# A hand-written order of 1100 steps replaced by another: a gated mix of a long convolution and an MLP on one core

## The chip, the core and the metric

The kernel runs on one core of a Trainium2 chip. The core has five instruction streams of its own: TensorE (PE; its weight loads appear as PEld), VectorE (DVE), ScalarE (ACT), GpSimd (POOL) and SyncE (SP, which here issues nearly all DMAs). Each works through its own list in the order in which the program put it there, and waits by semaphores for the results of the others. The metric is the time on the device in microseconds (us), the median of the runs; a profile is one execution, and its span runs from the first instruction to the last.

## The reference

Inputs are bf16; S = 2048 positions, D = 640 channels, F = 1536. `q` serves as `x` for the second branch.

```python
def _A_ref(q, k, v, shift_k, ssm_k, ssm_D):
    k_pad = jnp.pad(k, ((0, 0), (ks - 1, 0), (0, 0)))
    for t in range(ks):                      # ks = 4
        k_shift = k_shift + k_pad[:, t:t + S, :] * shift_k[:, ks - 1 - t][None, None, :]
    kv = k_shift * v
    # y: convolution of kv with ssm_k along S, by FFTs of length 2*S
    y = y + kv * ssm_D[None, None, :]
    return q * y

def _B_ref(x, w1, w2, w3, w4):
    h = _gelu(_layernorm(x, axis=-1) @ w1)
    # four channel groups of h are shifted by +1, -1, +2, -2 positions -> hs
    x1 = x + hs @ w2
    return x1 + _gelu(_layernorm(x1, axis=-1) @ w3) @ w4

g = _sigmoid((x * gate_w).sum(-1, keepdims=True))
return g * a + (1 - g) * b
```

## The kernel before

Positions are tiled as 128 partitions by 16 (t1), so that four "chunks" c hold four t1 each. Both branches go through TensorE, and their steps are interleaved.

Branch A. `k_load` brings a chunk of k, transposes it by matmul (tile `pst`) and copies it out of PSUM; `tap` does the four-tap shift as matmuls with diagonal weights and multiplies by v, which `v_load` gathers by an indirect DMA on POOL. The long convolution is an FFT in four matmul steps. `step1` (a 64-point transform, L407 to L434) is run for the signal (KV) and for the kernel of the convolution (HT0), four chunks each: its PSUM tiles are copied into `stg` and sent to DRAM scratch (S_x and S_h). `gather` (L436) reads the scratch back transposed into an `ax` tile, `step2` (L446) does the second transform into XS and hs, `product` (L478) multiplies the spectra, `step3` (L493) transforms back, copies to `gs` and sends to S_g, `gin` (L524) reads that, and `step4` (L877) finishes, with the gate and the factor q.

Branch B. `x_stats` and `x_norm` do the first LayerNorm (bn_stats on DVE, the power on POOL, `row_order` the index rows of v), `x_turn` transposes by matmul (A or V letters) or by a DMA transpose (D). `mlp1` multiplies by w1, one of its groups (u = 4) by a regrouped copy W1M that `w1_mixed` (L201) makes on DVE from both halves of w1 (`load_w1`, tile WA); gelu runs on ACT. `h_shift` and `w2` (L776), then `x1_norm` (L797) with DMA transposes, `w3` (L833) with gelu, `w4` (L857) and `store` (L848). `z_rows` and `gate` make the gate.

Where a result leaves PSUM, `evac` (L354) copies it: on ACT with letter A (L356), on DVE with letter V (L358). The letters are part of the name of a step: `step1.HT0.0.VAAVVAVAVV` evacuates its ten tiles in turn by V, A, A, V and so on. `step4` and the norms have such letters too.

Nothing is left to a scheduler. All five engines run in the order in which the string `ORDER` lists the steps: 1100 entries "name.arguments:k", the k-th step of the named routine. `emit` takes them one by one, and what a step issues goes to the end of its engine's list. A step can belong to one engine or hold a DMA; so the place of an entry matters only against the other entries of the same engine, and against what it depends on.

```python
    def emit(names):
        for e in names:
            n, k = e.split(":")
...
    with tc.manual_schedule(engines={getattr(mybir.EngineType, n) for n in ("PE", "DVE", "Activation", "Pool", "SP")}):
        emit(ORDER)
```

The rings of tiles are set by hand as well. `SLOTS` has one digit for each allocation of a ring: "c" are the eight PSUM banks, "row" the four rows that stg, xn, gs and q2 share, "ax" the four gather tiles, and so on. A step that takes a slot waits until the last reader of the slot's former tile is done.

Of the kernel before, what the change touches and what calls it, by code (L numbers as in the profile page):

```python
# [41 lines left out]
def kernel(  # L42
# [24 lines left out]
        "c": "012345670124703510347205142356401723605162370514731057423671045261304732641374153670421350627413"  # L67
             "502634751264351270361427503164257364102546173045621537426107432715604371401362570164301257613045"
             "267236057416537621507362651374026372401534762501373150427102547535706432073125640736450750634127"
             "504763270415367204325170635147630125460327156034215760147362304167135620316425031672301402715320"  # L70
             "1724107361761423564023714053627501267420674256271306234",
        "row": "01230213021302320123012031203120310310303",
        "gt": "012301031010231012301201",
        "xt": "010101",
        "gq": "0120201201021020120122102121021021",
        "ax": "0123120312030213",
        "hp": "01231302",
# [798 lines left out]
    def step4(t1, ev):  # L876
# [26 lines left out]
        def total():  # L903
# [170 lines left out]
                 f1_table=f1_table, t2_table=t2_table, i_tables=i_tables, f4_table=f4_table, kv_alloc=kv_alloc, k_load=k_load, k_wrap=k_wrap, v_load=v_load, tap=tap,  # L1074
                 kv_consts=kv_consts, mlp1=mlp1, load_h=load_h, h_transpose=h_transpose,
# [50 lines left out]
```

## Time and profile before

| | |
|---|---|
| median of 3 runs | 229.23 us (229.17 to 229.64) |
| span of the profiled execution | 225.9 us |
| around the span (median less span) | 3.3 us |
| instructions | 6037 |
| PE busy | 217.5 us, 96% of the span |
| DVE busy | 192.4 us, 85% |
| ACT busy | 173.0 us, 77% |
| POOL busy | 16.3 us, 7% |
| DMA | 57.62 MB, mean 255 GB/s |

The profiled execution has no time of its own beside its span; the median of the runs is taken for it. Busy times of PE are modelled: a matmul that is held up between two others counts as busy. Names such as `ps<-ax,CMP` mean output from inputs. A "releaser" is what ended a wait.

### The profile page before, as it was taken

Reading aid. Unit: us, or ns where it says so; the run is one execution under the profiler, and the core shown is the slowest. Engines: PE = TensorE matmul, PEld = TensorE weight load, DVE = VectorE, ACT = ScalarE, POOL = GpSimd, SP = SyncE. Lnnn points to the kernel's source line nnn. Section 1 sums busy time; section 2 is a strip of 40 time slices with the busy share of each in tenths; the row PEclk is TensorE's granted clock in tenths of the full one; section 3 lists DMA queues with packets and bytes.
Section 4 is the critical chain, followed back from the end, with each engine's and each line's share of the span. In section 5 each row is a group of like instructions: output and inputs, shape, how many; then the busy total and the mean of one; then the engine's idle time right before and its main releaser. Section 6 shows DMA issues by size and latency. Waiting matters only on the chain.

```text
span 225.9 us, 6037 instructions
## 1 busy us (share of the span) xinstructions
PE 217.5 (96%) x2419; PEld 120.4 (53%) x2420; DVE 192.4 (85%) x500; ACT 173.0 (77%) x344; POOL 16.3 (7%) x34
## 2 busy tenths in 40 slices
PE   8979989999999999999999999999999999999994
PEld 2557555436846554344664445555533547657762
DVE  7899999999999999873999998989999841439994
ACT  4799988989989989999977597967988450266450
POOL 3238020000000200010400000000000000000000
PEclk9999999999999999999999999999999999999999
DMA  6999997964998999999999560592695779418915
GB/s 238 381 362 336 308 249 193 344 282 104 392 352 353 307 240 290 376 361 369 300 250 303 121 232 4 156 361 70 69 323 195 219 269 372 189 30 321 310 77 197
DMA packets 43841, 57.62 MB, mean 255 GB/s; under 512 B 20514, under 2 KB 36514, under 8 KB 43558
## 3 DMA queue, kind: packets, MB, share of 16 engines
q1 hardware_dynamic: 43238, 54.62, 75.3%
q0 software_dynamic: 576, 2.62, 3.1%
q8 instruction: 19, 0.31, 0.6%
q14 instruction: 8, 0.07, 0.1%
HBM read 34.94 MB, written 18.36 MB: 236 GB/s over the span
## 4 chain that ended last, share of the span: by engine, by line
PE 63%; DMA 16%; DVE 15%; issue 1%; ACT 1%; SPq 1%; ACTq 0%
PE ps L864 23%; PE ps L837 18%; DMA WA<-in_B_w_dram 5%; DMA W<-in_B_w_dram 5%; PE ps L461 4%; PE ps L890 4%; PE psw L785 4%; PE psm L703 4%; DMA ax<-S_x 4%; PE ps L508 3%; DMA S_h<-stg 3%; PE ps L419 2%; DVE KV L601 2%; DVE KV L598 2%; DVE HT L358 2%; DVE HM L758 1%
## 5 line engine op out<-in xcount | busy, mean ns | idle before, releaser
L837 PE MATMUL ps<-x1t,W 128*128 128x512 bf16 x240 | 56.1, 380 | 0.0
L864 PE MATMUL ps<-W,gt 128*128 128x320 bf16 (+2 forms) x383 | 55.1, 299 | 0.6 <-DMA W<-in_B_w_dram 0.5
L864 PEld LDWEIGHTS <-gt 128*128 128x128 bf16 x384 | 36.2, 98 | 18.3 <-issue 2.8
L841 ACT ACTIVATE gt<-ps 128x512 bf16<-128x512 f32 x48 | 27.6, 609 | 19.0 <-PE ps L864 10.6
L837 PEld LDWEIGHTS <-W 128*128 128x128 bf16 x240 | 21.8, 98 | 28.2 <-issue 5.5
L356 ACT CAST stg<-ps 128x512 bf16<-128x512 f32 x55 | 28.6, 608 | 3.0 <-PE ps L419 1.8
L867 DVE SCALAR_TENSOR_TENSOR X<-ps,OMG,X 128x320 bf16<-128x320 f32 (+2 forms) x32 | 17.2, 548 | 11.9 <-PE ps L864 11.7
L703 PE MATMUL psm<-xt,WA 128*128 128x512 bf16 x100 | 23.4, 379 | 1.2 <-DMA WA<-in_B_w_dram 1.1
L356 ACT CAST gs<-ps 128x320 bf16<-128x320 f32 x41 | 15.6, 439 | 8.7 <-PE ps L508 5.2
L785 PE MATMUL psw<-WA,HT 128*128 128x320 bf16 x116 | 21.3, 299 | 0.2
L358 DVE CAST XS<-ps 128x512 bf16<-128x512 f32 x19 | 12.5, 684 | 5.3 <-PE ps L461 5.3
L356 ACT CAST hs<-ps 128x512 bf16<-128x512 f32 x28 | 15.0, 606 | 1.9 <-PE ps L461 1.9
L358 DVE CAST stg<-ps 128x512 bf16<-128x512 f32 x25 | 15.9, 683 | 0.2
L703 PEld LDWEIGHTS <-WA 128*128 128x128 bf16 x100 | 9.2, 97 | 12.0 <-DMA WA<-in_B_w_dram 1.2
L785 PEld LDWEIGHTS <-HT 128*128 128x128 bf16 x116 | 10.9, 98 | 7.7 <-issue 4.1
L894 ACT ACTIVATE y<-ps,GS 128x320 bf16<-128x320 f32 x22 | 10.4, 526 | 5.7 <-PE ps L890 3.5
L788 DVE SCALAR_TENSOR_TENSOR X<-psw,X 128x320 bf16<-128x320 f32 x32 | 14.2, 483 | 0.1
L358 DVE CAST gs<-ps 128x320 bf16<-128x320 f32 x23 | 10.7, 485 | 2.4 <-PE ps L508 1.7
L706 ACT ACTIVATE HT<-psm 128x512 bf16<-128x512 f32 x20 | 11.6, 618 | 1.2 <-PE psm L703 1.1
L356 ACT CAST XS<-ps 128x512 bf16<-128x512 f32 x21 | 11.9, 609 | 0.5 <-PE ps L461 0.3
L785 PE MATMUL psw<-WA,HM 128*128 128x320 bf16 x44 | 12.3, 299 | 0.0
L794 ACT ACTIVATE jk<-X 128x640 bf16<-128x640 bf16 x16 | 12.1, 759 | 0.0
(145 smaller groups left out, 334.8 us busy)
## 6 DMA issues: line engine op xcount, KB each, us to landing
S_x<-stg SPq DMA_DIRECT2D x8, 640.0 KB
S_h<-stg SPq DMA_DIRECT2D x8, 640.0 KB, 3.4
ax<-S_x SPq DMA_DIRECT2D x8, 640.0 KB, 8.1
ax<-S_h SPq DMA_DIRECT2D x8, 640.0 KB, 6.0
S_g<-gs SPq DMA_DIRECT2D x8, 640.0 KB, 3.6
W<-in_B_w_dram SPq DMA_DIRECT2D x2, 1920.0 KB
kn<-in_A_k_dram SPq DMA_DIRECT2D x4, 640.0 KB
E<-in_A_ssm_k_dram SPq DMA_DIRECT2D x5, 512.0 KB
```

The lines of the kernel that those rows point to most:

```text
L356: A.copy(out=dst, in_=src)
L358: V.tensor_copy(out=dst, in_=src)
L703: PE.matmul(ps[:].rearrange("p (a b) -> p a b", a=4), lhsT=W1N[:, k, 160 * u:160 * u + P] if u < 4 else W1M[:, k, :], rhs=xt[:, :, k, :], ...
L706: A.activation(out=st["HT"][:, 4 * c:4 * c + 4, u, :], in_=ps[:].rearrange("p (t b) -> p t b", t=4), func=ACT.Gelu_apprx_tanh)
L785: PE.matmul(ps[:], lhsT=h_tile(f, t1), rhs=W2P[:, f, o:o + W], start=(f == 0), stop=(f == 4))
L788: V.scalar_tensor_tensor(out=X1[:, t1, o:o + W], in0=box["ps"][:], scalar=1.0, in1=X[:, t1, o:o + W], op0=ALU.mult, op1=ALU.add, accum_out ...
L794: A.activation(out=jk[:], in_=X1[:, t1, :], func=ACT.Square, accum_out=S12[:, 1, t1:t1 + 1])
L837: PE.matmul(ps[:].rearrange("p (a b) -> p a b", a=4), lhsT=st["W3"][:, k, f * P:(f + 1) * P], rhs=xt[:, :, k, :], start=(k == 0), stop=(k ...
L841: A.activation(out=st["gt", c, f // 4][:, f % 4, :], in_=ps[:], func=ACT.Gelu_apprx_tanh)
L864: PE.matmul(ps[:], lhsT=st["gt", c, f // 4][:, f % 4, i * P:(i + 1) * P], rhs=st["W4"][:, f, o:o + w], start=(f == 0), stop=(f == FC - 1))
L867: V.scalar_tensor_tensor(out=X1[:, t1, o:o + w], in0=box["ps"][:], scalar=OMG[:, t1:t1 + 1], in1=X1[:, t1, o:o + w], op0=ALU.mult, op1=ALU ...
L894: A.activation(out=box["y"][:], in_=box["ps"][:], func=ACT.Copy, scale=GS[:, t1:t1 + 1])
```

## The change

The strings `ORDER` and `SLOTS` are replaced; all other lines are the same, but those behind ORDER move down by eight. The 1100 steps issue the same arithmetic and the same DMAs. What differs: the order on each of the five engines, the digits of the ring slots, and the letters of some steps, which move an evacuation between L356 (ACT) and L358 (DVE), a norm between ACT and DVE, or a step4 half between its two forms (L894 with L897, or L900). Counted over the whole program, DVE gets 39 copies of 128x512 in place of 44, 8 of step1.HT0's shape in place of 12 and 21 of 128x320 in place of 23. ACT gets four loads of its function table in place of five.

At the front, on POOL `v_load.1` and `v_load.3` now stand between the first power of `x_stats` and the second, `v_load.0` behind the second and `v_load.2` behind the third, where all four stood behind the second; `w1_mixed` comes forward to stand behind `x_stats.1`; w1, x2 and all of k are asked for early; `pow0` goes to the end. In the middle step1.HT0.1 and `load_w4` come earlier among the steps. At the end six step4 tiles (8 to 13) are finished directly before `w4.14`, the last product, and the stores 1, 7, 5, 6 and 4 lie among them.

The diff, cut to its core:

```diff
     SLOTS = {
...
-        "row": "01230213021302320123012031203120310310303",
-        "ax": "0123120312030213",
...
+        "row": "01023103302123013210321031331312301211210",
+        "ax": "0123102301232310",
...
     ORDER = (
-        "open.L1.left:0 open.A2.right:0 consts0:0 load_x0.0:0 warm:0 load_x0.1:0 consts0:1 warm:1 warm:2 pow0:0 "
-        "kv_alloc:0 k_load.3.AVA:0 f4_table:0 x_stats.0.VVVA:0 warm:3 k_load.3.AVA:1 x_stats.0.VVVA:1 load_x.1:0 "
-        "x_stats.0.VVVA:2 k_load.3.AVA:5 x_stats.0.VVVA:3 x_stats.0.VVVA:4 x_stats.0.VVVA:5 x_stats.0.VVVA:6 warm:4 "
-        "row_order:0 k_load.2.VAV:0 f1_table:0 x_norm.0.VVAA:0 x_norm.0.VVAA:1 f4_table:1 x_stats.1.VVVV:0 "
-        "k_load.3.AVA:2 load_x.3:0 x_norm.0.VVAA:2 x_stats.1.VVVV:1 k_load.3.AVA:3 x_turn.0.AAA:0 k_load.3.AVA:6 "
-        "k_load.2.VAV:5 load_w1.1:0 x_norm.0.VVAA:3 k_load.2.VAV:1 x_stats.1.VVVV:2 x_turn.0.AAA:1 x_stats.1.VVVV:3 "
-        "x_turn.0.AAA:2 x_stats.1.VVVV:4 load_w1.0:0 x_stats.1.VVVV:5 x_stats.3.VVAA:0 k_load.3.AVA:4 x_norm.1.VVVV:0 "
-        "x_turn.0.AAA:4 k_load.2.VAV:3 x_turn.0.AAA:3 x_turn.0.AAA:5 x_stats.3.VVAA:1 x_norm.1.VVVV:1 x_norm.1.VVVV:2 "
-        "v_load.2:0 k_load.0.AAV:0 f1_table:1 mlp1.0.2:0 mlp1.0.3:0 x_norm.1.VVVV:3 v_load.0:0 k_load.1.AVV:0 "
-        "k_load.2.VAV:6 mlp1.0.0:0 load_x.2:0 x_stats.3.VVAA:2 x_turn.1.VVV:0 x_turn.1.VVV:4 mlp1.0.1:0 "
-        "x_stats.3.VVAA:3 x_turn.1.VVV:1 k_load.2.VAV:4 x_stats.3.VVAA:4 x_stats.3.VVAA:5 k_load.0.AAV:3 x_turn.1.VVV:5 "
-        "mlp1.0.3:1 x_stats.3.VVAA:6 x_turn.1.VVV:2 v_load.3:0 x_turn.1.VVV:3 k_load.1.AVV:3 w1_mixed:0 v_load.1:0 "
-        "mlp1.0.0:1 x_stats.2.VVAA:0 mlp1.0.2:1 k_load.0.AAV:1 mlp1.0.1:1 x_stats.3.VVAA:7 k_load.0.AAV:5 mlp1.1.2:0 "
-        "x_norm.3.VVVV:0 x_norm.3.VVVV:1 k_load.0.AAV:4 load_cj:0 k_load.0.AAV:2 mlp1.1.2:1 x_norm.3.VVVV:2 "
-        "x_norm.3.VVVV:3 x_stats.2.VVAA:1 k_load.1.AVV:5 mlp1.0.4:0 k_load.1.AVV:4 mlp1.0.4:1 k_load.1.AVV:1 d_fold:0 "
-        "mlp1.1.4:0 x_turn.3.D:0 kv_consts:0 x_stats.2.VVAA:2 mlp1.1.0:0 k_load.2.VAV:2 k_wrap:0 k_load.1.AVV:6 "
...
-        "step2.x.3.AVVVVVAAVA:7 step2.x.0.VAVVAVAAVA:10 w3.0.11:1 w3.0.3:1 step1.HT0.1.VVAAAAAAVA:15 x1_norm.1.VVAA:3 "
...
-        "step2.x.3.AVVVVVAAVA:8 load_w4:0 w3.0.1:1 scale_x1.4.V:0 step2.x.0.VAVVAVAAVA:12 w3.0.2:1 w3.0.8:1 "
...
-        "step4.9.VV:2 w4.15:0 step4.11.AA:2 step4.12.AA:0 step4.10.AA:3 step4.14.AV:4 step4.14.AV:1 step4.8.VA:1 "
-        "load_q.3:0 step4.14.AV:5 step4.11.AA:5 step4.14.AV:2 store.1:0 step4.13.AA:0 store.2:0 step4.12.AA:3 "
-        "step4.8.VA:2 step4.15.AA:5 step4.15.AA:1 step4.14.AV:6 step4.15.AA:2 step4.12.AA:1 step4.10.AA:4 store.0:0 "
-        "step4.9.VV:6 step4.13.AA:3 step4.12.AA:2 step4.13.AA:4 step4.10.AA:0 step4.8.VA:4 step4.10.AA:5 store.3:0 "
-        "w4.13:2 step4.11.AA:6 w4.15:1 step4.12.AA:4 step4.13.AA:5 w4.15:2 step4.8.VA:5 w4.13:3 step4.10.AA:1 "
-        "step4.8.VA:6 step4.10.AA:2 step4.13.AA:1 step4.10.AA:6 w4.14:0 step4.13.AA:2 w4.15:3 step4.12.AA:5 store.4:0 "
-        "step4.13.AA:6 store.5:0 step4.15.AA:6 step4.12.AA:6 store.7:0 store.6:0 w4.14:1 w4.14:2 w4.14:3 store.8:0 "
-        "store.8:1 close.L2:0 close.C:0"
+        "open.L1.left:0 open.A2.right:0 consts0:0 kv_alloc:0 warm:0 consts0:1 f4_table:0 f4_table:1 row_order:0 "
+        "load_x0.0:0 x_stats.0.VVVA:0 load_x0.1:0 load_x.3:0 x_stats.0.VVVA:1 k_load.0.VAV:0 warm:1 "
+        "x_stats.0.VVVA:2 warm:2 warm:3 warm:4 load_x.1:0 x_stats.0.VVVA:3 x_stats.0.VVVA:4 f1_table:0 "
+        "k_load.0.VAV:5 k_load.2.AAV:0 x_stats.0.VVVA:5 k_load.0.VAV:3 x_stats.0.VVVA:6 load_w1.0:0 "
+        "x_stats.3.VVAA:0 x_stats.3.VVAA:1 x_stats.3.VVAA:2 x_stats.3.VVAA:3 load_w1.1:0 k_load.0.VAV:1 "
+        "x_stats.3.VVAA:4 x_stats.3.VVAA:5 x_norm.0.VAAA:0 x_stats.1.VVVV:0 x_norm.0.VAAA:1 x_norm.0.VAAA:2 "
+        "load_x.2:0 k_load.3.VAV:0 x_stats.1.VVVV:1 x_stats.1.VVVV:2 k_load.1.AVV:0 d_fold:0 x_stats.1.VVVV:3 "
+        "x_turn.0.AAA:0 k_load.2.AAV:5 v_load.1:0 load_cj:0 x_norm.0.VAAA:3 w1_mixed:0 k_load.2.AAV:1 "
+        "x_stats.1.VVVV:4 x_turn.0.AAA:1 v_load.3:0 k_load.0.VAV:2 x_turn.0.AAA:4 x_turn.0.AAA:5 x_turn.0.AAA:2 "
+        "x_turn.0.AAA:3 k_load.2.AAV:3 k_load.2.AAV:4 k_load.0.VAV:4 f1_table:1 mlp1.0.0:0 mlp1.0.0:1 "
+        "x_stats.1.VVVV:5 mlp1.0.4:0 x_stats.3.VVAA:6 x_stats.2.VVAA:0 x_norm.1.VVVV:0 x_norm.1.VVVV:1 "
+        "x_norm.1.VVVV:2 x_norm.1.VVVV:3 v_load.0:0 mlp1.0.2:0 mlp1.0.2:1 mlp1.0.4:1 load_h.0:0 k_load.3.VAV:5 "
+        "k_load.3.VAV:6 x_stats.2.VVAA:1 k_load.0.VAV:6 x_turn.1.VAV:0 x_turn.1.VAV:1 x_turn.1.VAV:4 x_turn.1.VAV:5 "
+        "k_load.2.AAV:2 x_stats.2.VVAA:2 x_stats.3.VVAA:7 x_norm.3.VVVV:0 x_norm.3.VVVV:1 x_norm.3.VVVV:2 "
+        "x_norm.3.VVVV:3 kv_consts:0 load_gw:0 x_turn.1.VAV:2 x_turn.1.VAV:3 x_stats.2.VVAA:3 x_stats.2.VVAA:4 "
+        "k_load.3.VAV:1 k_load.3.VAV:2 x_turn.3.D:0 x_stats.2.VVAA:5 x_stats.2.VVAA:6 k_load.1.AVV:1 v_load.2:0 "
...
+        "step2.x.3.VVVAVAAVAV:9 x1_norm.1.VVVA:2 step1.HT0.1.AAVVAVAAAA:15 w3.0.7:1 scale_x1.2.V:0 "
...
+        "step2.x.3.VVVAVAAVAV:5 x1_norm.1.VVVA:5 load_w4:0 w4.0:0 w4.3:0 step2.x.3.VVVAVAAVAV:4 "
...
+        "step4.2.AV:3 step4.6.AV:2 step4.6.AV:6 step4.2.AV:4 gin.1.1:0 gin.1.0:0 step4.2.AV:5 store.0:0 store.3:0 "
+        "w4.15:0 step4.15.VV:1 store.2:0 w4.15:1 step4.3.AA:3 step4.3.AA:4 step4.2.AV:6 step4.3.AA:5 w4.15:2 "
+        "step4.15.VV:2 step4.15.VV:6 step4.3.AA:6 w4.12:2 w4.15:3 w4.12:3 step4.10.AV:0 store.1:0 step4.10.AV:3 "
+        "step4.10.AV:4 store.7:0 step4.12.AA:3 step4.10.AV:1 step4.8.VA:0 step4.10.AV:5 step4.8.VA:1 step4.10.AV:2 "
+        "step4.8.VA:2 step4.11.AA:3 step4.12.AA:4 step4.12.AA:5 step4.11.AA:0 step4.10.AV:6 step4.11.AA:4 "
+        "step4.11.AA:5 step4.12.AA:0 step4.9.AA:3 step4.11.AA:1 step4.11.AA:2 step4.12.AA:1 step4.12.AA:2 "
+        "step4.11.AA:6 step4.13.AA:0 store.5:0 step4.13.AA:1 step4.13.AA:2 step4.12.AA:6 step4.9.AA:0 step4.8.VA:3 "
+        "step4.13.AA:3 step4.13.AA:4 step4.13.AA:5 step4.9.AA:1 step4.9.AA:2 step4.13.AA:6 store.6:0 step4.8.VA:4 "
+        "step4.8.VA:5 step4.9.AA:4 step4.9.AA:5 step4.8.VA:6 step4.9.AA:6 store.4:0 w4.14:0 w4.14:1 w4.14:2 "
+        "store.8:0 w4.14:3 store.8:1 close.L2:0 close.C:0"
     ).split()
```

More of the change, by code (lines that the diff above doesn't have):

```diff
@@ L66 @@
     SLOTS = {
[L67 to L71, printed above, removed]
-        "row": "01230213021302320123012031203120310310303",
-        "gt": "012301031010231012301201",
-        "xt": "010101",
-        "gq": "0120201201021020120122102121021021",
-        "ax": "0123120312030213",
-        "hp": "01231302",
+        "c": "012034567373207230175236075104632571023647601574231635410276451730207453215646054317234053721604"
+             "165704150742063145273604123106425731750436120716274306251643510723570416256201547364532156360172"
+             "714601421645030162714367406314254160327320150137613457275436245613157060142537127630145467236717"
+             "632021453520616240357137056564170324037156573120401465230541726713474641237612450241354351506270"
+             "2516056073751540613470132546301256075670617056170261570",
+        "gt": "000010223300203102301201",
+        "row": "01023103302123013210321031331312301211210",
+        "xt": "011101",
+        "gq": "012012020220210202222102102102",
+        "ax": "0123102301232310",
+        "hp": "01232031",
     }
```

280 rows, old and new, of the table ORDER are left out of this document.

## The prediction

> **What bounds the kernel now.** I read the page's first lines, then the busy time by stages, then the chain, and only then single stretches.
>
> ```profile
> span 225.9 us, 6037 instructions
> ...
> PE 217.5 (96%) x2419; PEld 120.4 (53%) x2420; DVE 192.4 (85%) x500; ACT 173.0 (77%) x344; POOL 16.3 (7%) x34
> ...
> PE 63%; DMA 16%; DVE 15%; issue 1%; ACT 1%; SPq 1%; ACTq 0%
> ```
>
> The median is 229.23 us and the span 225.9, so some 3.3 us lie around the span; I add them to every sum. "PE 96%" tempts one to say that TensorE bounds all of it and that no new order can matter. The chain says otherwise: 31% of the span goes back to DMA and DVE. The windows (span, then busy us and count of PE, PEld, DVE, ACT, POOL, then granted clock, DMA share, GB/s) show where:
>
> ```profile
> 0.00:10.00 10.00, 8.92 (x38) 3.75 (x39) 7.88 (x41) 5.65 (x9) 3.53 (x15) 1.00 0.80 303
> 10.00:30.00 20.00, 17.74 (x269) 11.73 (x270) 19.09 (x64) 19.94 (x38) 6.60 (x9) 1.00 1.03 321
> 30.00:60.00 30.00, 29.18 (x478) 16.75 (x466) 28.79 (x86) 26.53 (x52) 1.32 (x2) 1.00 0.78 260
> 60.00:78.00 18.00, 17.69 (x129) 9.78 (x127) 17.57 (x61) 16.86 (x33) 1.21 (x2) 1.00 0.91 337
> 78.00:90.00 12.00, 11.88 (x79) 6.41 (x77) 11.74 (x39) 11.18 (x23) 0.00 (x0) 1.00 1.09 277
> ...
> 180.00:200.00 20.00, 20.00 (x150) 11.42 (x149) 6.94 (x16) 5.08 (x11) 0.00 (x0) 1.00 0.66 247
> ```
>
> From 10 to 90 us DVE is busy 77.2 of 80 us: it sets the pace there, with ACT close behind. After that PE is the fullest, and from 180 to 200 DVE and ACT have almost nothing to do. PE's busy time before 90 us is stretched: a matmul that waits for its PSUM bank between two others counts as busy. So I put PE on an axis of its own work instead.
>
> ```profile
> 3.55 11.11 DMA WA<-in_B_w_dram
> 14.70 3.41 PE psm L703 x15
> 18.11 0.67 PE pst L615 x12
> 18.78 1.08 PE psm L703 x5
> ...
> 126.72 1.63 PE ps L864 x12
> ...
> 222.12 1.02 DVE X L867 x2
> ```
>
> Unhindered, five matmuls of L703 take 1.08 us and twelve of L864 1.63 (start, length, what, in the chain); likewise for the other forms. Counted over the order, PE's work is 206.5 us, the same in both programs. The last matmul ends at 222.1, so PE has lost 222.1 − 206.5 = 15.7 us by then, and DVE and stores add 3.8. The loss grows unevenly: by the row of 14.70 it is 3.0 us; at the w3 group at 87.14 (axis 77.6) it is 9.5; at the first w4 matmul, 105.71, it is 12.1; the rest comes in small pieces.
>
> ```profile
> 86.60 0.60 PE L419 MATMUL ps<-HT,F 64*128 64x512 bf16 x4
> 87.14 1.25 PE L837 MATMUL ps<-x1t,W 128*128 128x512 bf16 x5
> ...
> 105.71 0.58 PE L864 MATMUL ps<-W,gt 128*128 128x320 bf16 x3 [0.51 <-DMA W<-in_B_w_dram]
> ```
>
> The 9.5 have a simple reading. Around axis 79 PE needs results that stand behind 6.3 us more DVE work than PE has done itself; what remains, 9.5 − 6.3 = 3.2 us, is time that DVE idled on the way (2.1 of it before 10 us, by the first window). So the loss at that point is DVE work ahead plus DVE idle time, and these two I follow into the changed order.
>
> **The change part by part.** The instructions are the same but for the engines of some evacuations.
>
> *Evacuations moved.* DVE copies 11 tiles fewer out of PSUM at L358 (stg, XS, hs, gs), ACT as many more at L356. With the smaller exchanges of letters, each at its row's mean, DVE loses 5.9 us of work and ACT gains 3.7; ACT also drops one of five table loads.
>
> ```profile
> L356 ACT CAST stg<-ps 128x512 bf16<-128x512 f32 x55 | 28.6, 608 | 3.0 <-PE ps L419 1.8 <-ACT jk L794 0.7 <-DMA S_h<-stg 0.3
> ...
> L358 DVE CAST stg<-ps 128x512 bf16<-128x512 f32 x25 | 15.9, 683 | 0.2
> ```
>
> Most of that falls after 100 us, where the evacuations run beside PE and cost nothing. What counts is the DVE work ahead of PE in the paced part. There the tightest point becomes w3.0.6 at axis 77.1, which needs w2.14 behind 82.7 us of DVE work: 5.6 ahead, where it was 6.3. That is −0.7. ACT, in exchange, gets 32 of the 40 evacuations of step1.HT0, where it had 28 (step1.HT0.0 alone goes from 4 to 9), and its own work ahead of PE goes from 0.1 us at axis 59.5 to 0.9 at 78.2. While DVE is 5.6 ahead and late besides, ACT is covered; I count 0, and the four moved copies at 608 ns, 2.4 us, as the other end if that cover goes (second rival).
>
> *The front.* Now v_load.1 and v_load.3 stand on POOL right behind the first pow, ahead of the second, and w1_mixed stands on DVE right after x_stats.1.
>
> ```profile
> 7.45 1.03 POOL L653 TENSOR_TENSOR RS<-VE,EXPO 128x4 f32<-128x4 f32 x1 [4.55 <-DVE pf L256]
> ...
> 16.07 1.20 POOL L172 DMA_INDIRECT KV<-in_A_v_dram,ROWS  x1 [0.17 <-issue]
> ```
>
> The traffic of queue 0 (packets, MB, share), what the trace has on the tile of W1 (WA), and the use of W1 on DVE:
>
> ```profile
> q0 software_dynamic: 576, 2.62, 3.1%
> ```
> ```profile
> L196 SPq DMA_DIRECT2D WA<-in_B_w_dram x2: 939/1206/1474, 3.5 to 4.5; - x2
> ...
> DMA to landing us min/median/max: 11.2/11.2/11.2
> ```
> ```profile
> 21.41 0.32 DVE L202 COPY WA<-WA 128x640 bf16<-128x640 bf16 x1
> ```
>
> So these gathers start at about 10 us instead of 16 (the pow ends at 8.5, ROWS takes 0.3, a gather 1.2). Each moves a quarter of 2.62 MB, and at the 321 GB/s of 10 to 30 us two of them are 4.1 us of traffic. W1's halves are issued at 3.5 and 4.5 and take 11.2 us, so they land at 14.7 and 15.7 and are under way just then. In the old order w1_mixed ran at 21.41, long after W1; in the new one it stands behind 13.6 us of DVE work, so with the idle 2.1 it is reached at 15.7, when W1 has only just come by the old timing. DVE then waits between 0 (W1 served first) and 4.1 us (the gathers served first). I take 2.3, an even sharing: over the 4.6 us that follow 10 us, half goes to the gathers. Behind w1_mixed on DVE wait the x_norm, tap and evacuation work of the whole paced part, so this idle time adds directly to 3.2: it is **+2.3**. x2, k3 and k1 are all issued early and share the same engines; their lateness lies inside the same bounds.
>
> [...]
>
> *W4 and the first gathers.*
>
> ```profile
> 94.93 1.41 SPq L215 DMA_DIRECT2D W<-in_B_w_dram  x1
> ```
> ```profile
> 92.53 0.59 PE L837 MATMUL ps<-x1t,W 128*128 128x512 bf16 x2
> 93.24 0.85 PE L461 MATMUL ps<-ax,CMP 64*32 64x384 bf16 x48
> ```
>
> W4 is issued at 94.93 behind S_h sends that end step1. In the new order that last step1 and W4's issue come about 2 us earlier against PE, so the 0.51 wait goes (end of the row at 105.71). Between the two rows at 92.53 and 93.24 PE also loses some 0.3 us (two matmuls of L837 need 2 × 1.08/5 = 0.43 of the 0.71) to the first gather of S_x, which the new order issues earlier too: −0.8 in all, 0 to −0.8. The S_h gathers behind it get tighter. Between the release of an ax slot and its first use PE has 5.4 us of work for h.6, 6.2 for h.0, 6.5 for x.4, 7.6 for h.7 and 8.3 for h.5, where all had 7.9 to 13.8 before. A gather takes this long:
>
> ```profile
> DMA to landing us min/median/max: 6.0/7.0/8.1
> ```
>
> At 6.0 only h.6 is short, by 0.6; at 7.0 h.6, h.0 and x.4 are short by 1.6 + 0.8 + 0.5 = 2.9. PE stretches a little in that time, so I take **+1.0** (0 to 2.9).
>
> *The tail.* Six step4 tiles now stand right before w4.14: 12 half tiles, 3.3 us of PE, and 10 of them go over ACT:
>
> ```profile
> L894 ACT ACTIVATE y<-ps,GS 128x320 bf16<-128x320 f32 x22 | 10.4, 526 | 5.7 <-PE ps L890 3.5 <-DVE q L897 1.9
> ```
>
> That is 5.3 us of ACT against 3.3 of PE. Up to eight PSUM banks absorb the difference; the last w4 may wait for one: **+0.3** (0 to 1). The last step3 and its sends end about 5 us later than before (190 against 185), which the nearly empty DVE and ACT of 180 to 200 cover; first use is at about 200.
>
> Sum: −0.7 + 2.3 − 0.8 + 1.0 + 0.3 = +2.1, and 225.9 + 2.1 + 3.3 = 231.3 us. PE's work of 206.5 is equal in both, so a loss can come back only by less lag, and the paced part sets that.
>
> **The rivals.**
> *The front holds (faster).* W1 lands at 14.65 and 15.7 as before, because the gathers get what is left. Then w1_mixed waits for nothing, the −0.7 and −0.8 stand, the S_h gathers cost 0 to 0.6 (the lower landing time), and the tail 0 to 0.3: −1.5 to −0.6, 227.7 to 228.6; if a tenth of the 5.9 us that DVE sheds shortens the path elsewhere (from 60 to 78 us DVE is busy 17.57 of 18), 227.2. For it: the DMA engines in the first window are busy only 0.80. Against it: from 10 to 30 us it is 1.03 already. It decides if W1's second half lands before 15.7. Chance 0.27.
> *ACT becomes the bound.* From 60 to 78 us ACT is already busy 16.86 of 18 us, so it has 1.1 to spare, and two of the four moved copies fill that. If the front has held it as well, the whole 2.4 stands behind DVE's lateness and not beside it: 231.3 + 2.4 = 233.7. For it: 19.94 busy of 20 from 10 to 30. Against it: a late DVE gives ACT time. Chance 0.22.
> *Nothing comes of it.* The evacuations of the paced part wait for PE and the other way round, so shifts are taken up, so that PE's 206.5 meets about the old lag: the gains (−1.5) against a half-sized front (+1.2) give 228.9, within 0.45 of before. Chance 0.06.
> The forecast, 229.8 to 232.5 by the front's 0.8 to 3.5, keeps 0.45.
>
> **How the numbers follow.** A difference of 0.2% (0.45 us) is what a measurement can tell here. Faster takes the first rival, 0.27; the same 0.06; slower is the forecast and the ACT rival, 0.67. The range runs from the low end of the first rival, 227.2, to the ACT rival with part of what the gather term (2.9 instead of 1.0) or W1 (4.1 instead of 2.3) can add, 235.0. The forecast's own range stands above.
>
> **What would show it.** Right: DVE waits 1.5 to 3 us for WA at L202 near 16 us; the first w4 matmul comes without a wait for W, PE waits for ax appear at L461 for S_h gathers, the lag at the w3 group of axis 77 is 10 to 11 us. Wrong: no DVE wait at L202, and a lag there under 9 (first rival); ACT busy over 17.5 of 18 us in the stretch before that group with DVE waiting for ACT (second); a last matmul at 222 with all of these (third). Above all it would be wrong if a transfer that I took as early is late in a stage I counted as covered, such as S_g before 200 us.

## The result and the profile after

The changed kernel takes 237.47 us, the median of 4 runs (236.37 to 238.2), against 229.38 us (229.17 to 229.64) for the kernel before: a ratio of 1.0347, 95% interval 1.0311 to 1.0383. The forecast was 231.3 us with a range up to 235.0. The direction was right, the size was not. The profiled execution took 237.79 us.

The first lines of the page of the changed kernel, its granted clock in 40 slices, and the chain by engine:

```profile
span 236.0 us, 6047 instructions
...
PE 222.6 (94%) x2420; PEld 122.3 (52%) x2420; DVE 187.8 (80%) x489; ACT 176.9 (75%) x350; POOL 16.8 (7%) x34
...
PEclk9979999799999999999999999999999999999999
...
PE 73%; DMA 13%; DVE 9%; issue 2%; SPq 1%; DVEq 0%
```

The span is 10.1 us longer, the median only 8.1. Here 237.79 − 236.0 = 1.8 us lie around the span, and 1.7 to 1.9 in the other runs whose span and time are both on record, not the 3.3 that the prediction took from the median less the span. So the profiled execution of before was most likely faster than its median, by some 1.5 us, and as much of the differences between the two traces may be the spread of executions. The forecast is best compared as a span: 228.0 forecast, 236.0 measured.

The page already shows two things that the forecast did not hold: two slices in which the clock dips, and DVE, whose share falls by 5 points although its work falls by only 4.6 us. The prediction's axis, PE's own work, shows where the time goes. The table gives PE's lag behind that axis, worked out from the start of each group of matmuls in the two traces:

| axis, us of PE work | lag before | lag after | difference |
|---|---|---|---|
| 9.5 | 0.9 | 2.25 | 1.35 |
| 17 | 3.0 | 6.15 | 3.15 |
| 23 | 2.9 | 6.8 | 3.9 |
| 30 | 4.0 | 10.9 | 6.9 |
| 36 | 4.55 | 13.1 | 8.55 |
| 48 | 6.6 | 16.1 | 9.5 |
| 77 | 9.4 | 19.3 | 9.9 |
| 102 | 12.5 | 22.3 | 9.8 |
| 150 | 15.3 | 25.15 | 9.85 |
| 204 | 16.1 | 25.8 | 9.7 |

The whole loss is there before axis 77; behind it nothing is lost or won on balance. PE comes to axis 77 at some 96.2 us, in the kernel before at some 86 (its last window ends at 85.8, axis 76.4; DVE does not idle in between). Up to there the windows of the changed kernel (span, then busy us and count of PE, PEld, DVE, ACT, POOL, granted clock, DMA share, GB/s) are:

```profile
0.00:10.00 10.00, 9.01 (x43) 4.05 (x43) 7.88 (x41) 6.22 (x14) 1.87 (x12) 1.00 0.82 298
10.00:30.00 20.00, 16.20 (x140) 10.39 (x139) 16.93 (x58) 18.47 (x30) 8.63 (x12) 0.91 1.09 343
30.00:50.00 20.00, 16.81 (x443) 9.15 (x442) 14.40 (x33) 13.14 (x26) 0.38 (x2) 0.91 0.71 211
50.00:96.20 46.20, 45.06 (x332) 25.25 (x331) 42.85 (x143) 43.81 (x86) 1.21 (x2) 1.00 0.79 281
```

And the two later ones of the kernel before, up to the same point of the work (its first two stand in the prediction):

```profile
30.00:50.00 20.00, 19.18 (x370) 9.31 (x358) 19.12 (x61) 16.94 (x34) 1.32 (x2) 1.00 0.83 270
50.00:85.80 35.80, 35.37 (x292) 22.13 (x291) 34.91 (x112) 33.45 (x66) 1.21 (x2) 1.00 0.90 297
```

Span less DVE busy, window by window, is DVE's idle time: before 2.1, 0.9, 0.9 and 0.9, in all 4.8 us; after 2.1, 3.1, 5.6 and 3.35, in all 14.1. That is +9.3 of the +9.9 us of lag: +2.2 from 10 to 30 us, +4.7 from 30 to 50, +2.5 behind that. In 18 of the 19 traces of this study the span less DVE's idle time up to axis 77 lies between 221.1 and 222.9 us (in b_d40, which adds DVE work up to there, it is 223.8). This is bookkeeping and no cause, since the DVE work up to that point and the work behind it are nearly the same everywhere; but it says where to look: at what DVE waits for before axis 77.

The three stretches of it that the timeline of DVE shows best (start, length, instruction, idle time before it and what ended that):

```profile
15.51 0.29 DVE L202 COPY WA<-WA 128x640 bf16<-128x640 bf16 x1
...
25.80 0.83 DVE L549 TENSOR_TENSOR DG<-i,cr 128x640 bf16<-128x640 bf16 x1 [2.46 <-DMA cr<-in_A_shift_k_dram]
...
40.95 0.69 DVE L601 TENSOR_TENSOR KV<-psk,KV 128x512 bf16<-128x512 f32 x1 [3.02 <-PE psk L586]
```

The first row is where the forecast put its 2.3 us: w1_mixed waits for nothing. The second waits for `cr`, the few taps of shift_k, for 2.46 us. The third waits for the tap matmuls, and these wait themselves. The timeline of PE:

```profile
15.67 4.03 PE L703 MATMUL psm<-xt,WA 128*128 128x512 bf16 x15 [0.25 <-ACT xt L356]
...
34.87 0.28 PE L586 MATMUL psk<-DG,KT 32*128 32x128 bf16 x6 [0.52 <-issue]
...
40.52 0.73 PE L586 MATMUL psk<-DG,KT 32*128 32x128 bf16 x35 [2.62 <-issue]
```

"issue" means that nothing in the profile was being waited for. The two matmuls at 34.87 and 40.52 are PE's instructions number 707 and 963, counted from its first: 256 apart. The program's instructions come over a queue of their own:

```profile
q8 instruction: 19, 0.31, 0.6%
```

0.31 MB in 19 packets is 16 KB a packet, and PE's instructions, some 4860 with the weight loads, fill 19 blocks of 256; the five packets before 50 us begin 1.0 to 1.3 us after PE starts on such a block. So a packet is read here as one block for PE, an inference from these figures. In the trace's record of that queue a packet starts at 36.18, 1.3 us after PE entered the block before, and moves for 2.75 us, where the other four before 50 us take 0.93 to 1.14; 1.6 us after its end PE goes on. With a packet of 1.0 us that makes some 3.9 us for 256 instructions, an estimate from these figures. A tap issues 152 of them in 0.92 to 0.94 us. In the new order the taps stand close together, so PE seems to run dry; in the old order groups of mlp1 stand between them, and no wait of PE there names "issue".

### The profile page after: what moved, and what is told of

Same layout as the page of the kernel before. It is cut to its first block, busy times and chain, and to the rows that moved or that the text cites. A ratio compares the mean times of both kernels' runs of the same rounds, so it can differ in the third digit from the quotient of the medians.

```text
span 236.0 us, 6047 instructions
## 1 busy us (share of the span) xinstructions
PE 222.6 (94%) x2420; PEld 122.3 (52%) x2420; DVE 187.8 (80%) x489; ACT 176.9 (75%) x350; POOL 16.8 (7%) x34
## 3 DMA queue, kind: packets, MB, share of 16 engines
q0 software_dynamic: 576, 2.62, 2.8%
## 4 chain that ended last, share of the span: by engine, by line
PE 73%; DMA 13%; DVE 9%; issue 2%; SPq 1%; DVEq 0%
PE ps L837 23%; PE ps L864 19%; PE psw L785 9%; DMA cr<-in_A_shift_k_dram 6%; PE ps L461 4%; DMA kn<-in_A_k_dram 4%; PE ps L419 3%; PE psm L703 3%; DMA ax<-S_h 3%; PE ps L508 3%; PE psk L586 3%; PE ps L890 3%; PE pst L386 2%; DVE stg L358 2%; DVE HM L758 1%
## 5 line engine op out<-in xcount | busy, mean ns | idle before, releaser
L864 PE MATMUL ps<-W,gt 128*128 128x320 bf16 (+2 forms) x384 | 56.0, 299 | 0.1
L356 ACT CAST stg<-ps 128x512 bf16<-128x512 f32 x58 | 31.4, 619 | 1.9 <-PE ps L419 1.4
L703 PE MATMUL psm<-xt,WA 128*128 128x512 bf16 x100 | 24.4, 387 | 0.3 <-ACT xt L356 0.2
L356 ACT CAST gs<-ps 128x320 bf16<-128x320 f32 x43 | 15.9, 438 | 9.7 <-PE ps L508 9.4
L356 ACT CAST hs<-ps 128x512 bf16<-128x512 f32 x30 | 16.5, 607 | 1.6 <-PE ps L461 1.5
L788 DVE SCALAR_TENSOR_TENSOR X<-psw,X 128x320 bf16<-128x320 f32 x32 | 14.7, 487 | 2.9 <-PE psw L785 2.8
L894 ACT ACTIVATE y<-ps,GS 128x320 bf16<-128x320 f32 x20 | 9.7, 526 | 9.5 <-PE ps L890 8.0
L358 DVE CAST stg<-ps 128x512 bf16<-128x512 f32 x22 | 14.6, 685 | 2.8 <-PE ps L419 2.7
L356 ACT CAST XS<-ps 128x512 bf16<-128x512 f32 x25 | 14.0, 604 | 0.9 <-PE ps L461 0.8
L358 DVE CAST gs<-ps 128x320 bf16<-128x320 f32 x21 | 9.5, 485 | 6.3 <-PE ps L508 5.7
L461 PE MATMUL ps<-ax,CMP 64*32 64x512 bf16 (+3 forms) x512 | 12.2, 299 | 0.5 <-DMA ax<-S_h 0.5
L653 POOL TENSOR_TENSOR rn<-ve,EXPO 128x4 f32<-128x4 f32 x4 | 4.1, 1026 | 118.1 <-DVE ve L806 118.1
```

Source lines behind the costliest of these rows:

```text
L356: A.copy(out=dst, in_=src)
L358: V.tensor_copy(out=dst, in_=src)
L461: PE.matmul(ps[j][q:q + 32, lo - 512 * u:hi - 512 * u], lhsT=CMP[HALF[j], 8 * b + 4 * h + i, c, :], rhs=st[name, 2 * b + h][HALF[j], i, lo ...
L703: PE.matmul(ps[:].rearrange("p (a b) -> p a b", a=4), lhsT=W1N[:, k, 160 * u:160 * u + P] if u < 4 else W1M[:, k, :], rhs=xt[:, :, k, :], ...
L788: V.scalar_tensor_tensor(out=X1[:, t1, o:o + W], in0=box["ps"][:], scalar=1.0, in1=X[:, t1, o:o + W], op0=ALU.mult, op1=ALU.add, accum_out ...
L864: PE.matmul(ps[:], lhsT=st["gt", c, f // 4][:, f % 4, i * P:(i + 1) * P], rhs=st["W4"][:, f, o:o + w], start=(f == 0), stop=(f == FC - 1))
```

## The experiments

Each ratio is against the kernel before on the same chip, with its 95% interval. The kernel before had medians from 227.55 to 229.4 us on the chips used, and traces show one execution, which varies by some 1.5 us for kernels of the new order; so a difference of one or two us between two spans is weak evidence, and the intervals count more. The changed kernel was not run again beside the others, so setting its 1.0347 beside their ratios takes it that the ratio is the same on each chip. "after" and "before" in the headings tell which kernel is edited.

**Early gathers of v, put into the kernel before (b_v).**

```diff
 row_order:0
+v_load.1:0
+v_load.3:0
 k_load.2.VAV:0
...
-v_load.3:0
...
-v_load.1:0
```

> The kernel before with one move: v_load.1 and v_load.3 go behind the first power on POOL, as in the changed kernel, ahead of v_load.2 and v_load.0. The step of the prediction (the gathers take half of W1's rate): W1 lands 2 us later, PE's wait of 1.06 us at 14.7 grows to about 3, and the time rises by 1.5 to 2.5 us. Theory now (transfers land nearly in the order of their issue, so that what is issued behind the gathers is late and W1, ahead of them, is not): W1 lands within 0.5 us of 14.7, k0, k1, x2 and the shift filter land 2 to 4 us later, and the time changes by 0 to +1 us.

Measured 231.56 us, 1.0185 [1.0111, 1.0259]. This one edit is worth +4 us in the kernel before (2.5 to 5.9 by the interval), more than either theory gave it, and not by W1. The timeline of DVE has this wait:

```profile
24.33 0.89 DVE L681 BATCH_NORM_STATS2 b<-X 128x6 f32<-128x320 bf16 x2 [3.37 <-DMA X<-in_A_q_dram]
```

W1 landed at 13.54 and 14.67 by the trace, ahead of the 14.7 and 15.7 of the prediction; x2, issued behind, landed at 24.3 instead of 20.4. So here the early gathers pushed back what had yet to move, not what was already under way.

**The same two gathers moved back in the kernel after (a_v).**

```diff
-v_load.1:0
...
-v_load.3:0
...
 x_norm.1.VVVV:3
+v_load.1:0
+v_load.3:0
 v_load.0:0
```

> The changed kernel with one move on POOL: v_load.1 and v_load.3 go back behind the second power. Theory A2 (from 10 to 28 us the DMA engines are full and serve what was issued roughly in its order, so 1.3 MB of v, needed from 32 us on, keep k1, the shift filter and others from their readers; moving only the filter passed the wait on to k1): k1 lands by 19.5 instead of 22.9, the filter by 21 instead of 25.7, the 2.5 us of DVE wait at L549 and the 1.0 us of PE wait for kn are gone, and the time falls by 2.5 to 4 us, to a ratio of 1.017 to 1.024. Rival (the evacuation letters and PE's new order in the first 50 us cost the time, the DMA waits only fill it): ratio above 1.030.

Measured 234.01 us, 1.0244 [1.0198, 1.029]: an interval that lies below that of the changed kernel. The window and the row of DVE that waited for cr:

```profile
10.00:30.00 20.00, 17.32 (x193) 11.46 (x197) 18.57 (x63) 19.19 (x30) 8.57 (x13) 0.91 1.07 332
```
```profile
24.28 0.82 DVE L549 TENSOR_TENSOR DG<-i,cr 128x640 bf16<-128x640 bf16 x1
```

DVE idles 1.4 us there instead of 3.1, and the wait for cr is gone: it landed 8.0 us after its issue, not 13.8. The place of the two gathers is worth 2.4 us of the changed kernel's span (236.0 to 233.6), and by the ratios as much.

**Only cr issued earlier (a_cj).**

```diff
+load_cj:0
 load_x.2:0
...
 v_load.1:0
-load_cj:0
```

> The changed kernel with one DMA moved: the 5 KB of the shift filter (load_cj) are issued ahead of x2, k3 and k1 instead of behind them. In the changed kernel they land 13.8 us after issue, at 25.7, and DVE waits 2.5 us for them at L549. Theory A (small transfers that stand late in SP's order are the loss, as DVE paces what follows): the wait at L549 is gone, the taps start about 2.5 us earlier and the time falls by 1.5 to 2.5 us, to 235.0 to 236.0. Rival (PE's supply of instructions in the taps, and DVE's and PE's other waits, set the pace there): the wait goes, but PE only comes earlier to its stall in the taps, and the time falls by less than 0.7 us.

Measured 236.72 us, 1.0387 [1.0307, 1.0467]: no gain that the interval shows. The wait for cr is gone, but the next transfer in the row of issues is then late. PE's waits:

```profile
PE pst L615 <- DMA kn<-in_A_k_dram: 4.6, 2, 3.4
```

That is 4.6 us in two waits for k, where the changed kernel has 1.0. DVE's idle time falls only from 14.1 to 11.8. Taking away one late transfer did not help here, as the next in line was needed at the same time.

**The two big loads before the stall (a_h, a_he, a_cjh).** h.3 and h.1 (some 512 KB each) go out just before the slow packet. a_h issues them later, a_he earlier, and a_cjh is a_h with a_cj.

```diff
 # a_h
-load_h.3:0
...
-load_h.1:0
...
 load_w2:0
+load_h.3:0
+load_h.1:0
```

> The changed kernel with two DMAs moved: two of the 512 KB chunks of the filter (load_h.3, load_h.1) go from 34.8 us to behind the loads of w2 at about 45 us. In the changed kernel PE stands still for 2.62 us from 37.9 with no semaphore to blame, 256 instructions behind a shorter stop at 34.4, while a 16 KB packet of the instruction queue takes 2.75 us beside these chunks. Theory B (PE waits for its own instructions, whose fetch is slowed by the chunks): the packet takes about 1.1 us, the stall shrinks to under 1 us and the time falls by 1.5 to 2.5 us, to 235.0 to 236.0. Rival (dense taps use up instructions faster than any fetch brings them, or PE waits for something else): the stall stays at over 2 us and the time moves by less than 0.5 us.

> Both moves together. Theories A and B: the gains add, 3.5 to 5 us, to 232.5 to 234.0. If one wait takes the place of the other: 1.5 to 2.5 us as with one alone.

```diff
 # a_he
 load_h.2:0
+load_h.3:0
+load_h.1:0
...
-load_h.3:0
...
-load_h.1:0
```

> The changed kernel with load_h.3 and load_h.1 moved forward on SP, right behind load_h.2, ahead of the second DMA transpose, so that they have landed when the instruction packet of 36 us is fetched, and nothing of branch A's sends is behind them. Theory B2 (the fetch beside these chunks costs 2.6 us; when the chunks went behind w2 they took the same from the S_x sends): stall under 1 us, S_x sends as in the changed kernel, time down by 1.5 to 2.5 us, ratio 1.024 to 1.029. Rival (x_turn.2's transpose gets behind the chunks and z_rows waits, or the next wait takes the place): ratio above 1.031.

a_h took 238.2 us, 1.041 [1.0331, 1.0488]; a_cjh 237.18, 1.0362 [1.0279, 1.0445]; a_he 236.69, 1.0358 [1.0306, 1.0411]. None differs from the changed kernel's 1.0347. With the loads later the big stall falls from 2.62 to 0.7 us, so their place bears on it; but PE then waits for a copy by ACT, and cr comes late again (waits of PE, then of DVE, in a_h):

```profile
PE ps L419 <- ACT stg L356: 3.0, 1, 3.0
```
```profile
DVE DG L549 <- DMA cr<-in_A_shift_k_dram: 3.8, 1, 3.8
```

The windows of a_h show what became of DVE's idle time:

```profile
10.00:30.00 20.00, 14.93 (x132) 10.01 (x133) 15.67 (x55) 17.71 (x29) 7.44 (x11) 0.91 1.10 338
30.00:50.00 20.00, 19.01 (x463) 9.72 (x461) 18.14 (x47) 16.04 (x31) 1.38 (x2) 1.00 0.65 192
50.00:97.70 47.70, 44.37 (x320) 24.92 (x319) 40.59 (x133) 41.18 (x80) 1.21 (x2) 0.93 0.78 279
```

From 30 to 50 us it is 1.9 instead of 5.6, as if the stall had held DVE up there; but it is 4.3 instead of 3.1 ahead of that, with cr late, and 7.1 instead of 3.35 behind.

With the loads earlier the stall does not go; it grows to 4.0 us in one piece.

**Both early moves together (a_vhe), and an earlier first power (a_vhep).** a_vhe is a_v with a_he. a_vhep adds a move of f1_table's first step (four small DVE instructions) behind the first statistics, so that POOL's first power need not wait for it.

```diff
 # a_vhep, beside a_vhe's edits
-f1_table:0
...
 x_stats.0.VVVA:6
+f1_table:0
```

> Both moves. If A2 and B2 hold and add: 4 to 6 us less than the changed kernel, ratio 1.008 to 1.017. If one takes the other's place: as a_v alone.

> Both moves, and the four DVE steps of f1_table:0 (1.3 us) go behind the statistics of x0, so that the first power starts at about 8 us instead of 9.36. Theory: PE's wait of 1.5 us for the first x_norm at 11.6 falls to under 0.5; since DVE and ACT are full there, 0 to 1.3 us of it come through, ratio 1.004 to 1.015. Rival (W1 and k set the start of mlp1): no gain over both moves.

238.84 us, 1.0411 [1.0348, 1.0474], and 238.53, 1.0453 [1.0405, 1.0502]: both lose what a_v had gained. PE's first wait in a_vhe, and the one that took the place of the wait for xn in a_vhep:

```profile
PE psk L586 <- issue: 6.2, 2, 5.1
```
```profile
PE pst L615 <- DMA kn<-in_A_k_dram: 1.7, 1, 1.7
```

The long stall in a_vhe has another form than the first one: its packet moves for 1.19 us only, but it starts 5.4 us after PE entered the block before, at 39.37, not 1.3 us after. So the 3.9 us above are no upper limit.

**The stall itself (a_t), also with a_v (a_vt) and with later warm-up matmuls (a_vtw).** Three groups of mlp1 are put between the taps, as the kernel before has them, with PSUM banks to fit. a_vtw moves two steps of dummy matmuls closer to the first real ones.

```diff
 mlp1.0.1:1
+mlp1.3.1:0
+mlp1.3.1:1
 tap.1.VVAA:0
...
 mlp1.3.0:1
+mlp1.3.4:0
+mlp1.3.4:1
 tap.0.AVAV:0
+mlp1.3.3:0
+mlp1.3.3:1
...
 # a_vtw besides
-warm:3
-warm:4
...
 load_w1.1:0
+warm:3
+warm:4
```

> The changed kernel with three groups of mlp1 (3.1, 3.4, 3.3, five matmuls of 512 columns and 1.08 us each) moved forward on PE and ACT in between the taps, in banks that are free there; nothing else moves. Theory C: PE gets its instructions in packets of 256, each asked for only when PE enters the packet before it, and one takes about 1.3 us to start, 1.1 to move and 1.5 to be used, 3.9 us in all; a tap is 152 instructions in 0.94 us, so two taps with one mlp1 between run dry, and moving DMAs only moves the stall. With the three groups between, the stalls of PE at L586 with no releaser (3.1 us) fall to under 0.8, and the time falls by 1.5 to 3 us, ratio 1.022 to 1.028. Rival (the filter, landing at 25.7, and DVE set the pace, PE's stall is slack): ratio above 1.031.

> The same together with v_load.1 and v_load.3 behind the second power (a_v, 1.0244). Theory A2 + C: the gains add, ratio 1.009 to 1.017. Rival: no better than a_v, 1.022 to 1.027.

> As a_vt, with the last six warm-up matmuls (1.3 us) moved between the transposes of k0, so that PE idles less before the first x_turn at 11.6. Theory D (the granted clock of 0.83 from 10 to 20 us is the answer to PE's idle time before and costs 0.8 us in the first mlp1 groups): the clock stays 1.00 in that stretch and 0.3 to 1 us are gained over a_vt. Rival: the clock follows the thin load after 10 us, not these 1.3 us, and nothing is gained.

237.92 us, 1.0358 [1.0311, 1.0404]; 236.37, 1.0307 [1.027, 1.0344]; 238.56, 1.0363 [1.0312, 1.0414]. In a_t PE's waits that name "issue" fall from 3.1 to 0.7 us, and at axis 31 its lag is 8.0 us instead of 11.75. At axis 42 it is 14.6, as in the changed kernel. The window of a_t:

```profile
30.00:50.00 20.00, 17.76 (x455) 9.40 (x454) 13.90 (x31) 14.31 (x27) 0.17 (x1) 1.00 0.69 205
```

DVE idles 6.1 us there, no less than before the edit. PE did other work in the time of the stall, but not the taps on which DVE's next instruction waits. So the edit fills PE's time without bringing the taps forward, and a_t cannot tell what the stall costs DVE; it does show that idle PE time by itself is not the price. a_vt and a_vtw gain nothing over a_v (1.0244), so the two gains do not add. The clock is 1.00 from 10 to 50 us in a_vt already, so a_vtw says nothing on the warm-up matmuls.

**Is DVE's time at that place the price? (b_d40, b_d190).** Four memsets of DVE on an unused tile, in the kernel before, at about 44 us and at about 195 us. Nothing uses their output.

```diff
+    def dummy():
+        for _ in range(4):
+            V.memset(DUM[:], 0.0)
+        yield
...
 # b_d40
 tap.1.VAVA:4
+dummy:0
...
 # b_d190
 w3.3.8:1
+dummy:0
```

> The kernel before with four memsets of a scratch tile of 128x512 fp32 on DVE in front of the first step1 copies, near 44 us; nothing reads the tile. Their sum (about 1.2 to 2.4 us by the rows of smaller memsets) is to be read from the trace. DVE paces that part: the time rises by 80 to 110% of their sum. Rival (PE and ACT have the slack to take it up): by less than half of it.

> The kernel before with the same four memsets near 195 us, where DVE waits for PE most of the time. Theory: no change beyond 0.2%, so the same work costs its whole length in the paced part and nothing here.

The tile's row in b_d40:

```profile
L233 DVE MEMSET DUM<- x4: 485/485/485, 43.4 to 45.4; 128x512 f32 x4
```

These are 1.94 us of DVE. At 44 us they cost 3.3 us (231.47 against 228.18; 1.0147 [1.012, 1.0174]), at 195 us nothing (228.09; 1.0008 [0.9975, 1.0042]). In the first the clock also dips to 0.95 and 0.98 in the two windows from 30 us to axis 77, which can account for a part of what goes beyond 1.94. So lost DVE time before axis 77 is paid in full and more, above the 80 to 110% that were expected.

**Other DVE work into the hole (a_f, a_f2), and both with a_v (a_vf, a_vf2).** t2_table and h_shift stand behind the waiting products in the new order. They go ahead of them; a_f also takes i_tables along. Slots are set to fit.

```diff
 # a_f2; a_f puts i_tables:0 behind h_shift.0:0 too
 mlp1.3.0:1
+t2_table:0
+t2_table:1
...
 load_h.4:0
+h_shift.1:0
+h_shift.0:0
 step1.KV.3.VAVAAAAVAV:3
...
-h_shift.1:0
...
-h_shift.0:0
...
-t2_table:0
...
-t2_table:1
```

> The changed kernel with DVE work brought forward into DVE's idle time at the taps: t2_table:0 and :1 (3.0 us, needed only at step2) in front of tap.0's multiplications, i_tables:0 and two h_shift copies (1.3 us) in front of the first step1 evacuations. PE, ACT's copies and all DMAs keep their order. If DVE's idle time before axis 77 is the cause: 2.5 to 4 us of 14.1 go, and the span and the time fall by the same, ratio 1.017 to 1.025. If PE's stall at the taps itself, or ACT, sets the time: less than 0.7 us.

> The same together with v_load.1 and v_load.3 behind the second power. Cause is DVE's idle time: 11.9 us fall to 8 to 9.5, ratio 1.008 to 1.014. Otherwise as a_v, 1.022 to 1.027.

a_f took 244.52 us, 1.0731 [1.0693, 1.0769], and a_vf 243.25, 1.0649 [1.0613, 1.0684], both far slower. DVE in a_f:

```profile
55.18 0.23 DVE L264 TENSOR_SCALAR ag<-R,sm 128x8 f32<-128x8 f32 x1 [7.10 <-DMA Zs<-zr]
```

The tile of i_tables takes the slot that the rows zr had, so it waits until they have been sent. So the edit brings a wait of its own, and prices the mechanism once more: with this wait of 7.1 us the span is 245.0 instead of 236.0, a part of it by the clock, which is 0.94 behind 50 us instead of 1.00. Without i_tables:

> As a_f, but i_tables:0 stays where it was: only t2_table:0 and :1 (3.0 us) and two h_shift copies (0.5 us) come forward into DVE's idle time at the taps. DVE's idle time as the cause: of 14.1 us before axis 77, 2 to 3 go, the span falls by as much, ratio 1.021 to 1.027. If PE's stall sets the time: within 0.7 us of the changed kernel, ratio 1.031 to 1.038.

> The same with v_load.1 and v_load.3 behind the second power. DVE's idle time as the cause: 9 to 10.5 us of idle time before axis 77, ratio 1.011 to 1.018. Otherwise as a_v, 1.022 to 1.027.

a_f2 took 234.32 us, 1.0286 [1.0237, 1.0335], a_vf2 234.47, 1.0297 [1.0255, 1.0338]. The window of a_f2:

```profile
30.00:50.00 20.00, 17.43 (x453) 9.11 (x451) 19.36 (x49) 14.36 (x28) 1.38 (x2) 1.00 0.72 221
```

DVE idles 0.6 us where it idled 5.6, the clock does not dip, and the span is 232.9, 3.1 less. (The first stretch was 1.1 us worse in this execution, and the one behind 50 us 1.0.) The time gains less: the interval of a_f2 overlaps that of the changed kernel (1.0311 to 1.0383) and reaches into the ranges of both theories, so it does not decide between them. With a_v's edit on top, the two windows are:

```profile
10.00:30.00 20.00, 16.94 (x161) 10.68 (x159) 18.11 (x61) 19.87 (x34) 8.80 (x13) 1.00 1.06 329
30.00:50.00 20.00, 16.83 (x443) 8.57 (x442) 17.59 (x42) 13.57 (x27) 0.00 (x0) 0.91 0.85 234
```

That is 1.9 and 2.4 us of idle time: what the front gains, the middle loses again, and the sum (10.8 us up to axis 77, with 11.2 for a_f2 and 11.9 for a_v) hardly moves, and the time is no better than a_v's. None of the kernels beats the one before.

## Why the prediction was right in sign and wrong in size

*Right: where to look.* "Loss is DVE work ahead plus DVE idle time" must hold wherever both are measured up to the same point, so it proves nothing by itself. What the traces add is which of the two moved: at axis 77 they give 4.6 ahead and 4.8 idle before, 5.2 and 14.1 after. The −0.7 for evacuations moved away from DVE is not to be seen (+0.6), but it is small. The split that the prediction began from was off: its own windows give 2.1 + 2.8 = 4.9 us of DVE idle time up to 90 us, not 3.2, so there were not 6.3 us of work ahead.

*Right in size, in part by luck: what comes behind.* The first w4 matmul starts without a wait for W, and the S_h gathers show one wait (timeline and waits of PE in the changed kernel):

```profile
114.35 2.88 PE L864 MATMUL ps<-W,gt 128*128 128x320 bf16 x20
```
```profile
PE ps L461 <- DMA ax<-S_h: 0.5, 1, 0.5
```

The difference in lag moves by −1.3 across the w4 stage's start (forecast −0.8) and by +1.1 over the gathers (+1.0), of which this wait is 0.5. The end adds 0.4 (+0.3), but not by the forecast step: no wait of PE shows there. The chain of the changed kernel is DVE's from 226.47 us on: its step4 work, and directly behind that the X of the last w4, which in the kernel before waited for PE:

```profile
231.43 0.81 DVE X L904 x2
232.24 0.66 DVE X L867
```

That this size fits is luck. The rival in which ACT becomes the bound stays open. These are two windows of the changed kernel:

```profile
60.00:78.00 18.00, 17.22 (x150) 10.45 (x147) 17.37 (x51) 15.93 (x27) 0.00 (x0) 1.00 0.64 244
78.20:96.20 18.00, 18.00 (x129) 10.66 (x127) 15.83 (x60) 17.78 (x40) 1.21 (x2) 1.00 0.93 327
```

In the first ACT is busy 15.93 of 18 us, less than the 16.86 before. In the second, which is the stretch before the w3 group of axis 77, it is busy 17.78, over the 17.5 that the prediction named as the sign, and DVE only 15.83. The other half of the sign is missing: DVE's waits there name PE (1.3 us in 5 waits for w2's results, 0.6 for step1), none names ACT. No run tests it. The rival in which the front holds was right in its condition (W1 was not late) and wrong in its time.

*The step that failed: DVE's idle time.* The prediction carried the old 3.2 us over and added one new wait, 2.3 us for W1. Measured up to axis 77 it rose by 9.3 us (4.8 to 14.1), in three parts, and none is a wait for W1.

First, 10 to 30 us, +2.2. This is the size that was forecast, with the wrong transfer, so the agreement is luck. The gathers were taken to be under way from 10 us, beside W1. The packets of the changed kernel's queues (0 the gathers, 1 the loads of SP), first from 10 to 15.4 us and then from 15.4 to 20, say otherwise:

```profile
q1 hardware_dynamic: 1581, 2.04, 107.3%
...
q0 software_dynamic: 205, 0.97, 51.2%
q1 hardware_dynamic: 208, 0.94, 49.7%
```

Issued at 10.85 and 12.31, the gathers moved nothing before 15.4 us, and from then on took half, as forecast. W1's halves had landed by then, at 13.04 and 14.49. What the gathers delayed was what still stood in SP's queue, whether issued before them or after: of k1, issued at 9.5, PE had to wait until 22.96, and cr landed at 25.7. Why they began so late no run shows. The chain of the changed kernel goes over two loads of the front (start, us, what), of which only the second, cr, was still to move by then:

```profile
3.12 8.73 DMA kn<-in_A_k_dram
11.87 13.84 DMA cr<-in_A_shift_k_dram
```

The prediction had said of x2, k3 and k1 that their lateness lies inside W1's bounds; cr it did not mention. For W1 itself its bounds were 0 and 4.1 us; the row at 15.51 shows no wait at all, but since W1 and the gathers never moved side by side, how they would have shared was not shown. The gathers landed at 19.91 and 23.32. b_v and a_v show the price of their place from both sides (+4 us in, −2.4 us out).

Second, 30 to 50 us, +4.7, with no term in the sum. In the new order DVE reaches the tap products early, against PE, with t2_table and h_shift queued behind; it takes its list in order, so here a delay of PE's taps is idle time of DVE (3.02 us before the product at 40.95). PE's taps were delayed, by the front, by the stalls read as waits for instructions, and by the clock. The prediction counted DVE work ahead at axis 77 alone, where DVE is still ahead of PE's need; it never asked where, on the way there, DVE would have to wait for PE. In the traces this window's idle time goes from 5.6 to 0.6 us when DVE has other work to do (a_f2) and to 1.9 when the long stall is gone (a_h), but neither brought the time down clear of noise, and a_f2's edit on top of a_v brought nothing. So the waiting for the taps is shown, and that the order of DVE's list is what costs here is argued. That was the question to ask of a reordering: not only what each engine does by the tightest point, but at each place whether the waiting one has something else ready.

Third, behind 50 us, +2.5, among it DVE's waits for w2's results (1.3 us in 5 waits up to axis 77, none before). It is there in a_v and a_f2 too, 3.3 and 4.4 us of idle time against 0.9. No experiment took it away; its cause stays open, with the full ACT of the window above as one candidate. Open, too, is how the second part splits between the front's lateness, the packets and the clock: edits of one moved the wait to another.

## What to carry to other kernels

When an order is changed under an engine that sets the pace, list for that engine every place where it will wait on the way and what stands ready behind the waiting instruction; a sum of its work up to the tightest point is only a lower bound. With the DMA engines full (a share of 1.09 from 10 to 30 us in the changed kernel) the two early gathers were paid for by the transfers that had yet to move when they began to: cr landed 13.8 us after its issue, and 8.0 with the two moved back (a_v). So price an early transfer by those next in line, the small ones too, and not by its time of issue. A wait that one edit removes is a gain only when the next one in line is later; here a load, a stall on "issue" and a copy took turns.

## What was not expected of the hardware

**PE stood still with nothing in the profile to wait for.** In a dense run of small matmuls there were stalls of 0.52 and 2.62 us, exactly 256 instructions apart, and one of 5.1 us in a_vhe, with "issue" as the releaser; PE went on from that of 2.62 us 1.6 us after a 16 KB packet of the instruction queue had ended. That PE ran out of instructions is the reading of these figures.

**Half the clock after steps with PE half idle.** In all 19 traces the granted clock is 1.0 or 0.5 and changes in steps of 3.41 us, on a grid that lies differently in each execution. These are windows on that grid, of the changed kernel around its two dips, then of a_cj:

```profile
10.15:13.56 3.41, 1.57 (x25) 1.40 (x26) 3.31 (x12) 3.36 (x6) 2.55 (x4) 1.00 1.09 355
13.56:16.97 3.41, 3.16 (x23) 2.18 (x21) 3.27 (x15) 3.41 (x5) 0.94 (x1) 0.50 1.02 410
...
37.45:40.86 3.41, 0.79 (x64) 0.62 (x52) 0.48 (x2) 0.21 (x1) 0.00 (x0) 1.00 0.64 253
40.86:44.27 3.41, 3.41 (x102) 2.06 (x87) 3.32 (x7) 1.66 (x3) 0.00 (x0) 0.50 0.25 76
```
```profile
17.04:20.46 3.42, 1.78 (x9) 0.59 (x6) 2.53 (x8) 3.39 (x7) 2.99 (x5) 1.00 1.02 414
20.46:23.87 3.41, 1.64 (x29) 1.64 (x30) 1.20 (x3) 2.34 (x6) 0.74 (x2) 1.00 1.02 409
23.87:27.28 3.41, 2.19 (x33) 1.78 (x31) 3.38 (x10) 3.22 (x6) 0.00 (x0) 1.00 0.78 257
```

After steps with PE busy 1.57 and 0.79 us the clock was halved for the next one. In a_cj PE stood still for 3.41 us in one piece, from 18.8 to 22.2, but this fell on two steps with 1.78 and 1.64 us busy, and the clock stayed whole. Up to 100 us, every step of these traces with PE busy 1.61 us or less was followed by a halved one; from 1.64 to 1.76 both occur, and above that it happened twice (1.93 in a_vt, and 2.57 in a_h in a step that was itself halved). So in these traces the halving goes with the busy time of the step before, and not with the longest single idle time: 3.41 us in a_cj did not halve the clock, and ahead of the second dip of the changed kernel it was 2.62 us. The fifteen mlp1 matmuls at 15.67 took 4.03 us instead of 3.24 (15 × 1.08 / 5), so here a late PE fell later still.
